# Attention spread between the matmuls of the FFN, in a fixed order, instead of all attention first

## The chip, the cores and the metric

The kernel runs on one core of one Trainium2 chip. The metric is the device time of one execution in microseconds; lower is better. Three runs of the kernel before are known, and one further execution was recorded by the profiler.

## The reference

The input has 4 batches, 8 heads, 768 positions and 64 channels a head, all fp32. Attention is linear, with a decay `lam` per head and a running state, and its result (3,072 tokens of 512 channels) goes through a bilinear FFN:

```python
for b in range(nb):                        # blocks of positions
    intra = einsum('bhic,bhjc->bhij', qb, kb) * Dmask      # Dmask: lam ** (i - j), 0 above the diagonal
    intra = einsum('bhij,bhjd->bhid', intra, vb)
    inter = einsum('bhid,bhde->bhie', qb * lam_pow, kv_state)
    out[:, :, sl] = intra + inter
    kv_state = lam_block * kv_state + einsum('bhsd,bhse->bhde', kb * rev_pow, vb)
...
x = out.transpose(0, 2, 1, 3).reshape(3072, 512)
return ((x @ w_a) * (x @ w_b)) @ w_out     # w_a, w_b: 512 x 1536, w_out: 1536 x 512
```

Both kernels take blocks of 128 positions and put the decay into the operands: q is scaled by `lam ** (pos + 1)` and k by `lam ** -(pos + 1)`, so that the mask is a plain triangle (`lotri`) and the state needs no decay.

## The kernel before

It has two stages, one after the other, and the framework's scheduler chooses the order of the instructions on each engine from the data they need and the buffers that are free.

The weights are loaded as fp32 by SyncE's queue (L88: four pieces of 768 KB each for `w_a` and `w_b`, twelve of 256 KB for `w_out`) and cast to bf16 by VectorE (L89). q, k and v are loaded by POOL's queue (L109 to L111), one DMA per batch, tensor and block of 128 positions, and cast from fp32 to bf16 by the DMA itself: it reads 256-byte rows (64 channels of one head and position) and writes 128-byte rows.

Attention then runs batch by batch. VectorE scales all q and all k of a batch (L115, L116, 3,072 elements a partition). TensorE transposes them in pairs of heads (L130, L131), and ScalarE copies eight transposes at once out of PSUM (L132). For each block and each pair of heads the inner loop multiplies k and q of one head (L152, `kq_ps`), VectorE masks the 128x128 result (L154), and TensorE adds up the block's own part (L156) and the state's part (L157) in `o_ps`; L158 makes the state's update, VectorE adds it to a bf16 state in SBUF (L160), and ScalarE copies `o_ps` into `xT_sb` (L161), which holds all 3,072 tokens. TensorE's matmuls of this loop have four shapes: 64x128, 128x64, 64x64 and again 128x64.

Last comes the FFN, for 6 groups of 512 tokens. For each of 12 chunks of 128 hidden channels TensorE does four matmuls into `a_ps` (L185) and four into `b_ps` (L188), all of 512 columns; ScalarE copies a (L191), VectorE multiplies it by b (L193), and four more matmuls (L195) add the chunk to four PSUM banks of output, open over all 12 chunks. At a group's end ScalarE copies the four banks into two SBUF buffers in turn (L199), and SyncE's queue stores them (L200).

Of the kernel before, what the change touches and what calls it, by code (L numbers as in the profile page):

```python
# [20 lines left out]


@with_exitstack
def kernel(
# [13 lines left out]
    assert D == 64  # L38
# [2 lines left out]
    d_model = moe_w_a.shape[0]
    d_ff = moe_w_a.shape[1]
# [1 line left out]
    assert d_model == H * D

    singles = ctx.enter_context(tc.tile_pool(name="singles", bufs=1))

    lam_bc = bass.AP(tensor=lam.tensor, offset=lam.offset, ap=[[0, 128], lam.ap[0]])
    lam_sb = singles.tile([128, H], F32, name="lam_sb")
    nc.sync.dma_start(out=lam_sb, in_=lam_bc)  # L50
# [27 lines left out]
    wa_sb = singles.tile([128, 4, d_ff], BF16, name="wa_sb")
    wb_sb = singles.tile([128, 4, d_ff], BF16, name="wb_sb")
    wo_sb = singles.tile([128, d_ff // 128, d_model], BF16, name="wo_sb")  # L80
    wtmp_pool = ctx.enter_context(tc.tile_pool(name="wtmp", bufs=3))
    for (src, dst, kdim, ndim) in ((moe_w_a, wa_sb, 4, d_ff),
                                   (moe_w_b, wb_sb, 4, d_ff),
                                   (moe_w_out, wo_sb, d_ff // 128, d_model)):
        src_r = src.rearrange("(ko p) n -> p ko n", p=128)
        for ki in range(kdim):
            wtmp = wtmp_pool.tile([128, ndim], F32, name="wtmp", tag="w")
            nc.sync.dma_start(out=wtmp, in_=src_r[:, ki, :])  # L88
            nc.vector.tensor_copy(dst[:, ki, :], wtmp)  # L89

    xT_sb = singles.tile([128, 4, N_TOK], BF16, name="xT_sb")

    qc = q.rearrange("b h (nb p) d -> b p nb h d", p=BLK)
    kc = k.rearrange("b h (nb p) d -> b p nb h d", p=BLK)
    vc = v.rearrange("b h (nb p) d -> b p nb h d", p=BLK)

    attn_ctx = ExitStack()
    bpool = attn_ctx.enter_context(tc.tile_pool(name="bpool", bufs=2))
    kvpool = attn_ctx.enter_context(tc.tile_pool(name="kvpool", bufs=2))
    blk_pool = attn_ctx.enter_context(tc.tile_pool(name="blk", bufs=4))  # L100
    psum1 = attn_ctx.enter_context(tc.tile_pool(name="psum1", bufs=1, space=bass.MemoryType.PSUM))
    psum2 = attn_ctx.enter_context(tc.tile_pool(name="psum2", bufs=2, space=bass.MemoryType.PSUM))

    for b in range(B):
        q_sb = bpool.tile([128, NB, H, 64], BF16, name="q_sb", tag="q")
        k_sb = bpool.tile([128, NB, H, 64], BF16, name="k_sb", tag="k")
        v_sb = bpool.tile([128, NB, H, 64], BF16, name="v_sb", tag="v")
        for nb in range(NB):
            nc.gpsimd.dma_start(out=q_sb[:, nb], in_=qc[b, :, nb])  # L109
            nc.gpsimd.dma_start(out=k_sb[:, nb], in_=kc[b, :, nb])  # L110
            nc.gpsimd.dma_start(out=v_sb[:, nb], in_=vc[b, :, nb])  # L111

        qs_sb = bpool.tile([128, NB, H, 64], BF16, name="qs_sb", tag="qs")
        ks_sb = bpool.tile([128, NB, H, 64], BF16, name="ks_sb", tag="ks")
# [2 lines left out]
        kv_sbs = []
        for hp in range(H // 2):
            kv = kvpool.tile([128, 64], BF16, name="kv", tag=f"kv{hp}")
            nc.vector.memset(kv, 0.0)  # L120
            kv_sbs.append(kv)

        qkT_all = bpool.tile([128, NB, 8, 128], BF16, name="qkT_all", tag="qkT")
        tr_ctx = ExitStack()
        psumT = tr_ctx.enter_context(tc.tile_pool(name="psumT", bufs=2, space=bass.MemoryType.PSUM))
        for nb in range(NB):
            tps = psumT.tile([128, 8, 128], BF16, name="tps", tag="T")
            for hp in range(H // 2):
                h0 = 2 * hp
                nc.tensor.transpose(tps[:, hp * 2, :], qs_sb[:, nb, h0:h0 + 2, :], ident)  # L130
                nc.tensor.transpose(tps[:, hp * 2 + 1, :], ks_sb[:, nb, h0:h0 + 2, :], ident)  # L131
            nc.scalar.copy(qkT_all[:, nb], tps)  # L132
        tr_ctx.close()

        for nb in range(NB):
            cols = slice(b * S + nb * BLK, b * S + (nb + 1) * BLK)
            for hp in range(H // 2):
                h0 = 2 * hp
                kv_sb = kv_sbs[hp]
                qT = qkT_all[:, nb, hp * 2, :]  # L140
                kT = qkT_all[:, nb, hp * 2 + 1, :]

                o_ps = psum2.tile([128, 128], F32, name="o_ps", tag="o")
                kvd_ps = psum1.tile([128, 64], F32, name="kvd_ps", tag="kvd")
                for i in range(2):
                    h = h0 + i
                    psl = slice(i * 64, (i + 1) * 64)
                    vb = v_sb[:, nb, h]
                    kb = ks_sb[:, nb, h]

                    kq_ps = psum1.tile([128, 128], F32, name="kq_ps", tag=f"kq{i}")
                    nc.tensor.matmul(kq_ps, lhsT=kT[psl, :], rhs=qT[psl, :], start=True, stop=True)  # L152
                    masked = blk_pool.tile([128, 128], BF16, name="masked", tag="msk")
                    nc.vector.tensor_mul(masked, kq_ps, lotri)  # L154

                    nc.tensor.matmul(o_ps[psl, :], lhsT=vb, rhs=masked, start=True, stop=False)  # L156
                    nc.tensor.matmul(o_ps[psl, :], lhsT=kv_sb[psl, :], rhs=qT[psl, :], start=False, stop=True)  # L157
                    nc.tensor.matmul(kvd_ps[psl, :], lhsT=kb, rhs=vb, start=True, stop=True)  # L158

                nc.vector.tensor_add(kv_sb, kv_sb, kvd_ps)  # L160
                nc.scalar.copy(xT_sb[:, hp, cols], o_ps)  # L161

    attn_ctx.close()

    fpsum = ctx.enter_context(tc.tile_pool(name="fpsum", bufs=1, space=bass.MemoryType.PSUM))
    ab_pool = ctx.enter_context(tc.tile_pool(name="ab", bufs=2))
    opool = ctx.enter_context(tc.tile_pool(name="opool", bufs=2))

    N_GROUP = 512
    NG = N_TOK // N_GROUP  # L170
    NT_SUB = N_GROUP // 128
    FF_CHUNKS = d_ff // 128
    K_SUB = d_model // 128
    out_r = out.rearrange("(g t p) n -> g t p n", p=128, t=NT_SUB)

    for g in range(NG):
        tok_sl = slice(g * N_GROUP, (g + 1) * N_GROUP)
        out_ps = [fpsum.tile([128, d_model], F32, name=f"out_ps{t}", tag=f"ops{t}")
                  for t in range(NT_SUB)]
        a_ps = fpsum.tile([128, N_GROUP], F32, name="a_ps", tag="aps")  # L180
        b_ps = fpsum.tile([128, N_GROUP], F32, name="b_ps", tag="bps")
        for f in range(FF_CHUNKS):
            fsl = slice(f * 128, (f + 1) * 128)
            for s in range(K_SUB):
                nc.tensor.matmul(a_ps, lhsT=wa_sb[:, s, fsl], rhs=xT_sb[:, s, tok_sl],  # L185
                                 start=(s == 0), stop=(s == K_SUB - 1))
            for s in range(K_SUB):
                nc.tensor.matmul(b_ps, lhsT=wb_sb[:, s, fsl], rhs=xT_sb[:, s, tok_sl],  # L188
                                 start=(s == 0), stop=(s == K_SUB - 1))
            a_sb = ab_pool.tile([128, N_GROUP], BF16, name="a_sb", tag="a")  # L190
            nc.scalar.copy(a_sb, a_ps)  # L191
            ab_sb = ab_pool.tile([128, N_GROUP], BF16, name="ab_sb", tag="ab")
            nc.vector.tensor_mul(ab_sb, a_sb, b_ps)  # L193
# [37 lines left out]
```

## Time and profile before

| | |
|---|---|
| median of 3 runs | 434.49 us (431.78 to 438.37) |
| span of the profiled execution, its own time | 432.4 us |
| TensorE matmuls busy | 362.2 us, 1,824 of them |
| VectorE, ScalarE, POOL busy | 163.2, 106.7, 66.5 us |
| DMA | 25.49 MB in 81,384 packets |

The profile gives no further time for the profiled execution than its span, from the first to the last instruction. The median of the runs lies 2.1 us above it. TensorE's busy time counts a matmul from its start to the end of its way through the array, so matmuls that overlap count as one stretch, and a busy TensorE isn't one at its peak: the distance between the starts of two matmuls tells more.

### The profile page before, as it was taken

To read this page: it belongs to the slowest core of one execution; us is meant where nothing else is said; L and a number is where in the kernel's file an instruction comes from. 1 tells how busy PE (TensorE), PEld (TensorE's weight loads), DVE (VectorE), ACT (ScalarE), POOL (GpSimd) and SP (SyncE) were. 2 spreads that over 40 slices of the span, in tenths; PEclk is the share of its full clock that TensorE was granted. 3 is DMA by queue.
4 is the path that set the end of the run, shared out by engine and by line. 5 is a ranking of instruction groups with operands and counts; after the bars stand their busy time and mean duration, and the time that the engine had idled before them with its cause. 6 is when DMAs were issued, how large, how long until landed. Compare 5 with 4: busy or idle time off the path is not lost.

```text
span 432.4 us, 4890 instructions
## 1 busy us (share of the span) xinstructions
PE 362.2 (84%) x1824; PEld 170.2 (39%) x1824; DVE 163.2 (38%) x406; ACT 106.7 (25%) x221; POOL 66.5 (15%) x81
## 2 busy tenths in 40 slices
PE   0000479957999999799999999999999999999993
PEld 0000345526655555455543333333333333333340
DVE  3325345588555555634432222222222222222220
ACT  3000411116511111151112213224224224213222
POOL 8458770049000400000000000000000000000000
PEclk9999999999555555555559999999999999999997
DMA  9999999059500920000000002002002002002002
GB/s 241 315 274 153 222 186 68 0 37 147 39 0 2 58 17 0 2 0 2 0 0 2 0 2 97 0 2 98 0 2 97 0 2 97 2 0 98 2 0 98
DMA packets 81384, 25.49 MB, mean 59 GB/s; under 512 B 75728, under 2 KB 75728, under 8 KB 81360
## 3 DMA queue, kind: packets, MB, share of 16 engines
q0 software_dynamic: 74880, 9.44, 35.6%
q1 hardware_dynamic: 6480, 15.74, 10.0%
q8 instruction: 14, 0.23, 0.2%
q14 instruction: 10, 0.08, 0.1%
HBM read 28.32 MB, written 6.29 MB: 80 GB/s over the span
## 4 chain that ended last, share of the span: by engine, by line
PE 80%; DMA 11%; DVE 3%; POOL 2%; issue 2%; ACT 1%; DVEq 0%; ACTq 0%; POOLq 0%
PE out_ps L195 17%; PE a_ps L185 15%; PE b_ps L188 15%; PE o_ps L157 10%; PE kq_ps L152 9%; PE o_ps L156 8%; DMA v_sb<-in_v_dram 4%; DMA wtmp<-in_moe_w_out_dram 4%; PE kvd_ps L158 4%; DMA k_sb<-in_k_dram 2%; PE tps L130 2%; DVE ks_sb L116 2%; PE tps L131 1%; ACT qkT_all L132 1%; POOL k_sb L110 1%
## 5 line engine op out<-in xcount | busy, mean ns | idle before, releaser
L193 DVE TENSOR_TENSOR ab_sb<-a_sb,b_ps 128x512 bf16<-128x512 bf16 x72 | 49.5, 688 | 151.5 <-PE b_ps L188 151.5
L191 ACT CAST a_sb<-a_ps 128x512 bf16<-128x512 f32 x72 | 42.2, 586 | 146.4 <-PE a_ps L185 146.4
L185 PE MATMUL a_ps<-xT_sb,wa_sb 128*128 128x512 bf16 x288 | 77.3, 386 | 0.3 <-DVE kv L160 0.3
L195 PE MATMUL out_ps<-wo_sb,ab_sb 128*128 128x512 bf16 x288 | 75.6, 382 | 1.2 <-DVE ab_sb L193 1.2
L188 PE MATMUL b_ps<-xT_sb,wb_sb 128*128 128x512 bf16 x288 | 74.8, 383 | 0.0
L154 DVE TENSOR_TENSOR masked<-kq_ps,lotri 128x128 bf16<-128x128 f32 x192 | 54.9, 291 | 46.1 <-PE kq_ps L152 45.3
L156 PE MATMUL o_ps<-masked,v_sb 128*64 128x128 bf16 x192 | 58.1, 302 | 4.8 <-DVE masked L154 4.8
L157 PE MATMUL o_ps<-qkT_all,kv 64*64 64x128 bf16 x192 | 59.6, 310 | 0.0
L130 PE MATMUL tps<-ident,qs_sb 128*128 128x128 bf16 x96 | 20.8, 293 | 45.0 <-DVE qs_sb L115 43.1
L152 PE MATMUL kq_ps<-qkT_all 64*128 64x128 bf16 x192 | 51.6, 283 | 0.4 <-DVE masked L154 0.4
L161 ACT CAST xT_sb<-o_ps 128x128 bf16<-128x128 f32 x96 | 25.5, 268 | 105.4 <-PE o_ps L157 105.4
L195 PEld LDWEIGHTS <-ab_sb 128*128 128x128 bf16 x288 | 22.4, 98 | 53.0 <-DVE ab_sb L193 35.6
L185 PEld LDWEIGHTS <-wa_sb 128*128 128x128 bf16 x288 | 28.4, 99 | 35.1 <-issue 1.6
L188 PEld LDWEIGHTS <-wb_sb 128*128 128x128 bf16 x288 | 28.4, 99 | 34.6 <-issue 1.1
L132 ACT COPY qkT_all<-tps 128x1024 bf16<-128x1024 bf16 x24 | 23.7, 1013 | 59.0 <-PE tps L131 58.9
L157 PEld LDWEIGHTS <-kv 64*64 64x64 bf16 x192 | 23.9, 124 | 27.1 <-issue 5.1
L111 POOL DMA_DIRECT2D v_sb<-in_v_dram x24 | 22.1, 931 | 65.5 <-PE o_ps L157 63.5
L156 PEld LDWEIGHTS <-v_sb 128*64 128x64 bf16 x192 | 26.6, 139 | 12.5 <-issue 1.5
L130 PEld LDWEIGHTS <-qs_sb 128*128 128x128 bf16 x96 | 12.4, 134 | 45.8 <-DVE qs_sb L115 43.2
L160 DVE TENSOR_TENSOR kv<-kv,kvd_ps 128x64 bf16<-128x64 bf16 x96 | 21.1, 220 | 24.1 <-PE o_ps L157 23.0
L131 PE MATMUL tps<-ident,ks_sb 128*128 128x128 bf16 x96 | 20.8, 297 | 9.9 <-DVE ks_sb L116 9.9
L152 PEld LDWEIGHTS <-qkT_all 64*128 64x128 bf16 x192 | 18.5, 102 | 21.6 <-issue 1.1
(28 smaller groups left out, 155.7 us busy)
## 6 DMA issues: line engine op xcount, KB each, us to landing
out_dram<-o_sb SPq DMA_DIRECT2D x24, 256.0 KB, 2.0
wtmp<-in_moe_w_a_dram SPq DMA_DIRECT2D x4, 768.0 KB, 7.2
q_sb<-in_q_dram POOLq DMA_DIRECT2D x24, 128.0 KB, 8.2
...
wtmp<-in_moe_w_out_dram SPq DMA_DIRECT2D x12, 256.0 KB, 6.0
lam_sb<-in_lam_dram SPq DMA_DIRECT2D x1, 4.0 KB, 2.7
```

Source lines behind the costliest of these rows:

```text
L130: nc.tensor.transpose(tps[:, hp * 2, :], qs_sb[:, nb, h0:h0 + 2, :], ident)
L132: nc.scalar.copy(qkT_all[:, nb], tps)
L152: nc.tensor.matmul(kq_ps, lhsT=kT[psl, :], rhs=qT[psl, :], start=True, stop=True)
L154: nc.vector.tensor_mul(masked, kq_ps, lotri)
L156: nc.tensor.matmul(o_ps[psl, :], lhsT=vb, rhs=masked, start=True, stop=False)
L157: nc.tensor.matmul(o_ps[psl, :], lhsT=kv_sb[psl, :], rhs=qT[psl, :], start=False, stop=True)
L161: nc.scalar.copy(xT_sb[:, hp, cols], o_ps)
L185: nc.tensor.matmul(a_ps, lhsT=wa_sb[:, s, fsl], rhs=xT_sb[:, s, tok_sl], start=(s == 0), stop=(s == K_SUB - 1))
L188: nc.tensor.matmul(b_ps, lhsT=wb_sb[:, s, fsl], rhs=xT_sb[:, s, tok_sl], start=(s == 0), stop=(s == K_SUB - 1))
L191: nc.scalar.copy(a_sb, a_ps)
L193: nc.vector.tensor_mul(ab_sb, a_sb, b_ps)
L195: nc.tensor.matmul(out_ps[t], lhsT=ab_sb[:, t * 128:(t + 1) * 128], rhs=wo_sb[:, f, :], start=(f == 0), stop=(f == FF_CHUNKS - 1))
```

## The change

The two stages become one. Attention works on units of one block of 128 positions with all 8 heads (24 units), and the units of the next 512 tokens are put between the FFN matmuls of the current 512 by a plan written out by hand; the scheduler is switched off (`manual_schedule`), so each engine's order is the program's order. Units 0 to 3 come before the first FFN matmul. The FFN of a group has two phases: first all a, b and products of the 12 chunks, kept in SBUF (`ab`), then for each 128 tokens 12 matmuls into one bank. A hook after each chunk (slots 0 to 11) and each half of an output tile (slots 12 to 19) issues the pieces of the next group's units.

q, k and v are loaded as fp32 by SyncE's queue, batch 0 block by block (256 KB), the others in one DMA per tensor. POOL scales q and k (for the first four units VectorE scales q), VectorE casts v (ScalarE for the first four). The weights come in nine chunks of 1 MB on the same queue, through three buffers, cast by VectorE, ScalarE and POOL. The state of a batch is added up in a PSUM bank of its own and copied to bf16 once per unit. One pool of seven PSUM banks serves everything else.

```diff
+    wst_pool = ctx.enter_context(tc.tile_pool(name="wst", bufs=3))
+    ld_pool = ctx.enter_context(tc.tile_pool(name="ld", bufs=2))
+    prep_pool = ctx.enter_context(tc.tile_pool(name="prep", bufs=4))
+    qkT_pool = ctx.enter_context(tc.tile_pool(name="qkT", bufs=3))
+    msk_pool = ctx.enter_context(tc.tile_pool(name="msk", bufs=2))
...
+    a_pool = ctx.enter_context(tc.tile_pool(name="a", bufs=3))
+    ab_pool = ctx.enter_context(tc.tile_pool(name="ab", bufs=2))
+    o_pool = ctx.enter_context(tc.tile_pool(name="o", bufs=4))
+    ps_pool = ctx.enter_context(tc.tile_pool(name="ps", bufs=7, space=PSUM))
+    kvps_pool = ctx.enter_context(tc.tile_pool(name="kvps", bufs=1, space=PSUM))
+
+    ctx.enter_context(tc.manual_schedule())
...
+    def load_batch(b, n0=0, n1=NB):
+        if b not in batch_tiles:
+            alloc_batch(b)
+        for t, src in zip(batch_tiles[b], (qr, kr, vr)):
+            if n0 == 0 and n1 == NB:
+                nc.sync.dma_start(out=t[:].rearrange("p h nb d -> p (h nb) d"),
+                                  in_=src[b].rearrange("p h nb d -> p (h nb) d"))
+            else:
+                for nb in range(n0, n1):
+                    nc.sync.dma_start(out=t[:, :, nb, :], in_=src[b, :, :, nb, :])
...
+    load_batch(0, 0, UPG)
+    load_w("a", 0)
+    load_w("b", 0)
+    load_w("a", 1)
...
-        nc.vector.tensor_mul(qs_sb, q_sb, lp_q_bc)
-        nc.vector.tensor_mul(ks_sb, k_sb, lp_k_bc)
+    def prep(u, first=False):
...
+        (nc.vector if first else nc.gpsimd).tensor_mul(qs, qf[:, :, nb, :], lq)
+        nc.gpsimd.tensor_mul(ks, kf[:, :, nb, :], lk)
+        if first:
+            nc.scalar.copy(vb, vf[:, :, nb, :])
+        else:
+            nc.vector.tensor_copy(vb, vf[:, :, nb, :])
...
+    def piece_T(u):
+        tps = ps_bank("tps", [128, 2, HP, 128], BF16)
+        for j, src in enumerate((d["qs"], d["ks"])):
+            for hp in range(HP):
+                nc.tensor.transpose(tps[:, j, hp, :], src[:, 2 * hp:2 * hp + 2, :], ident)
+        qkT = qkT_pool.tile([128, 2, HP, 128], BF16, name="qkT", tag="qkT")
+        nc.scalar.copy(qkT, tps)
+    def piece_KQ(u):
+        kq = [ps_bank(f"kq{i}", [128, HP, 128], F32) for i in range(2)]
+        for hp in range(HP):
+            for i in range(2):
+                p = slice(64 * i, 64 * i + 64)
+                nc.tensor.matmul(kq[i][:, hp, :], lhsT=qkT[p, 1, hp, :], rhs=qkT[p, 0, hp, :], ...
+        for i in range(2):
+            nc.vector.tensor_mul(m, kq[i], lotri_bc)
...
+    def piece_O(u, xT, col):
+        # hp, i: o_ps[p, hp] = vb (128x64) on m[i]; then, if nb > 0, += st (64x64) on qkT
+        nc.scalar.copy(xT[:, :, col:col + BLK], o_ps)
+        # if nb < NB - 1: hp, i: kvd[p, hp] += ks (128x64) on vb
+            nc.vector.tensor_copy(st, kvd)
...
+    def ffn(g, xT, hook):
+        ab = ab_pool.tile([128, FC, GT], BF16, name="ab", tag="ab")
+        for f in range(FC):
+            # 4 matmuls into a_ps, nc.scalar.copy(a_sb, a_ps), 4 into b_ps
+            nc.vector.tensor_mul(ab[:, f, :], a_sb, b_ps)
+            hook(f)
+        for t in range(UPG):
+            op = ps_bank("op", [128, d_model], F32)
+            for f in range(FC):
+                nc.tensor.matmul(op, lhsT=ab[:, f, t * 128:(t + 1) * 128], rhs=wo_sb[:, f, :],
+                                 start=(f == 0), stop=(f == FC - 1))
+                if f == FC // 2 - 1:
+                    hook(FC + 2 * t)
+            nc.scalar.copy(o_sb, op)
+            nc.sync.dma_start(out=out_r[g * UPG + t], in_=o_sb)
+            hook(FC + 2 * t + 1)
...
+    for u in range(UPG):
+        prep(u, first=True)
+    cast_w("a", 0, "dve")
+    cast_w("b", 0, "act")
+    load_w("b", 1)
+    load_w("a", 2)
+    load_batch(0, UPG, NB)
+    for step in range(UPG + 2):
+        if step < UPG:
+            piece_T(step)
+        if 0 <= step - 1 < UPG:
+            piece_KQ(step - 1)
+        if 0 <= step - 2 < UPG:
+            piece_O(step - 2, xTs[0], (step - 2) * BLK)
+    base = [0, 4, 9, 14]
+    offs = [(1, 2, 4), (1, 2, 4), (1, 2, 3), (1, 2, 3)]    # slots of T, K, O of the next group's four units
+    preps = {0: 0, 3: 1, 8: 2, 12: 3}
...
+            if g == 0:
+                if slot == 0:
+                    cast_w("a", 1, "dve")
+                    load_w("b", 2)
+                if slot == 1:
+                    cast_w("b", 1, "act")
+                    load_w("o", 0)
+                if slot == 3:
+                    cast_w("a", 2, "dve")
+                    load_w("o", 1)
+                if slot == 4:
+                    cast_w("b", 2, "act")
+                    load_w("o", 2)
+                    load_batch(1)
+                # slots 7, 9, 10: cast_w("o", 0 / 1 / 2, "pool")
+            if slot in preps:
+                u = nxt * UPG + preps[slot]
+                prep(u)
+                if u % NB == NB - 1 and u // NB + 2 < B:
+                    load_batch(u // NB + 2)
```

## Rows read from the trace of the kernel before

**Rows 1.** The page: span, and the chain that ended last, by engine.

```profile
span 432.4 us, 4890 instructions
...
PE 80%; DMA 11%; DVE 3%; POOL 2%; issue 2%; ACT 1%; DVEq 0%; ACTq 0%; POOLq 0%
```

**Rows 2.** Windows: stretch, length, busy us (count) per engine, granted clock, DMA share, GB/s.

```profile
0.00:40.40 40.40, 0.03 (x1) 0.03 (x2) 12.72 (x21) 3.26 (x5) 26.11 (x36) 1.00 1.60 252
40.40:223.50 183.10, 161.32 (x960) 90.92 (x960) 100.87 (x314) 48.75 (x120) 40.40 (x46) 0.69 0.64 48
223.50:228.80 5.30, 5.21 (x13) 1.92 (x14) 0.72 (x2) 0.59 (x1) 0.00 (x0) 0.50 0.00 0
229.00:425.60 196.60, 195.39 (x852) 77.31 (x850) 48.85 (x71) 52.37 (x93) 0.00 (x0) 1.00 0.07 27
425.60:432.40 6.80, 0.07 (x1) 0.00 (x0) 0.00 (x0) 1.71 (x4) 0.00 (x0) 0.60 0.41 155
```

**Rows 3.** Timeline of TensorE from 309.8 us: start, length, instruction.

```profile
309.89 1.03 PE L188 MATMUL b_ps<-xT_sb,wb_sb 128*128 128x512 bf16 x4
310.75 1.03 PE L185 MATMUL a_ps<-xT_sb,wa_sb 128*128 128x512 bf16 x4
311.77 0.60 PE L195 MATMUL out_ps<-wo_sb,ab_sb 128*128 128x512 bf16 x2
```

**Rows 4.** Timeline of TensorE from 45 us.

```profile
45.31 0.31 PE L130 MATMUL tps<-ident,qs_sb 128*128 128x128 bf16 x1
45.41 0.31 PE L131 MATMUL tps<-ident,ks_sb 128*128 128x128 bf16 x1
```

**Rows 5.** Timeline of TensorE from 102.6 us.

```profile
102.86 0.22 PE L131 MATMUL tps<-ident,ks_sb 128*128 128x128 bf16 x1
102.92 0.22 PE L130 MATMUL tps<-ident,qs_sb 128*128 128x128 bf16 x1
...
103.30 0.24 PE L157 MATMUL o_ps<-qkT_all,kv 64*64 64x128 bf16 x1
103.47 0.24 PE L156 MATMUL o_ps<-masked,v_sb 128*64 128x128 bf16 x1
...
103.81 0.23 PE L152 MATMUL kq_ps<-qkT_all 64*128 64x128 bf16 x2
103.97 0.23 PE L130 MATMUL tps<-ident,qs_sb 128*128 128x128 bf16 x1
```

**Rows 6.** Timeline from 223.5 us, the first matmuls of the FFN.

```profile
223.59 1.89 PE L185 MATMUL a_ps<-xT_sb,wa_sb 128*128 128x512 bf16 x4 [0.32 <-DVE kv L160]
...
225.27 1.91 PE L188 MATMUL b_ps<-xT_sb,wb_sb 128*128 128x512 bf16 x4
```

**Rows 7.** The page's costliest groups: busy us, mean ns of one, idle before and releaser.

```profile
L193 DVE TENSOR_TENSOR ab_sb<-a_sb,b_ps 128x512 bf16<-128x512 bf16 x72 | 49.5, 688 | 151.5 <-PE b_ps L188 151.5
L191 ACT CAST a_sb<-a_ps 128x512 bf16<-128x512 f32 x72 | 42.2, 586 | 146.4 <-PE a_ps L185 146.4
...
L132 ACT COPY qkT_all<-tps 128x1024 bf16<-128x1024 bf16 x24 | 23.7, 1013 | 59.0 <-PE tps L131 58.9
...
L111 POOL DMA_DIRECT2D v_sb<-in_v_dram x24 | 22.1, 931 | 65.5 <-PE o_ps L157 63.5
```

**Rows 8.** Groups of instructions by line, shapes apart: weight cast, POOL's select.

```profile
L89 DVE CAST wa_sb<-wtmp 128x1536 bf16<-128x1536 f32 x4 | 4.1, 1014 | 10.3 <-DMA wtmp<-in_moe_w_a_dram 10.3
...
L58 POOL TENSOR_SCALAR_AFFINE_SELECT lotri<-lotri 128x128 bf16<-128x128 bf16 x1 | 0.3, 294 | 0.0
```

**Rows 9.** DMA: window of weight loads; POOL's queue (packets, MB, share); store's landing.

```profile
4.00:8.00 4.00, 0.00 (x0) 0.00 (x0) 0.96 (x1) 1.03 (x1) 4.00 (x5) 1.00 1.02 383
...
q0 software_dynamic: 74880, 9.44, 35.6%
...
out_dram<-o_sb SPq DMA_DIRECT2D x24, 256.0 KB, 2.0
```

**Rows 10.** Timeline of the end: the last two copies and their wait.

```profile
427.95 1.20 ACT L199 COPY o_sb<-out_ps 128x512 f32<-128x512 f32 x2 [1.82 <-DMA out_dram<-o_sb]
```

More of the change, by code (lines that the diff above doesn't have):

```diff
@@ L37 @@
     B, H, S, D = q.shape
[L38 removed]
     BLK = 128
     NB = S // BLK
[L41 to L42 removed]
+    HP = H // 2
+    d_model, d_ff = moe_w_a.shape
+    assert D == 64 and d_model == H * D
     N_TOK = B * S
[L44 to L50 removed]
+    GT = 512
@@ L78 @@
[L78 to L114, printed above, removed]
-        nc.vector.tensor_mul(qs_sb, q_sb, lp_q_bc)
-        nc.vector.tensor_mul(ks_sb, k_sb, lp_k_bc)
[L117 to L144, printed above, removed]
-                for i in range(2):
[L146 to L174, printed above, removed]
-    for g in range(NG):
[L177 to L193, printed above, removed]
-            for t in range(NT_SUB):
-                nc.tensor.matmul(out_ps[t], lhsT=ab_sb[:, t * 128:(t + 1) * 128],
-                                 rhs=wo_sb[:, f, :], start=(f == 0), stop=(f == FF_CHUNKS - 1))
-        for t in range(NT_SUB):
-            o_sb = opool.tile([128, d_model], F32, name="o_sb", tag="osb")
-            nc.scalar.copy(o_sb, out_ps[t])
-            nc.sync.dma_start(out=out_r[g, t], in_=o_sb)
@@ new lines, in piece_O @@
+    def piece_O(u, xT, col):
+        b, nb = divmod(u, NB)
+        d = U.pop(u)
+        ks, vb, qkT, m = d["ks"], d["vb"], d["qkT"], d["m"]
+        o_ps = ps_bank("o_ps", [128, HP, 128], F32)
+        for hp in range(HP):
+            for i in range(2):
+                p = slice(64 * i, 64 * i + 64)
+                nc.tensor.matmul(o_ps[p, hp, :], lhsT=vb[:, 2 * hp + i, :], rhs=m[i][:, hp, :],
+                                 start=(hp == 0), stop=(nb == 0), skip_group_check=True)
+        if nb > 0:
+            st = kv_state[b]
+            for hp in range(HP):
+                for i in range(2):
+                    p = slice(64 * i, 64 * i + 64)
+                    nc.tensor.matmul(o_ps[p, hp, :], lhsT=st[p, hp, :], rhs=qkT[p, 0, hp, :],
+                                     start=False, stop=True, skip_group_check=True)
+        nc.scalar.copy(xT[:, :, col:col + BLK], o_ps)
+        if nb < NB - 1:
+            if nb == 0:
+                kv_state["ps"] = kvps_pool.tile([128, HP, D], F32, name="kvd", tag="kvd")
+            kvd = kv_state["ps"]
+            for hp in range(HP):
+                for i in range(2):
+                    p = slice(64 * i, 64 * i + 64)
+                    nc.tensor.matmul(kvd[p, hp, :], lhsT=ks[:, 2 * hp + i, :], rhs=vb[:, 2 * hp + i, :],
+                                     start=(nb == 0 and hp == 0), stop=True, skip_group_check=True)
+            st = kv_pool.tile([128, HP, D], BF16, name="st", tag="st")
+            nc.vector.tensor_copy(st, kvd)
+            kv_state[b] = st
@@ new lines @@
+    out_r = out.rearrange("(t p) n -> t p n", p=128)
+    def ffn(g, xT, hook):
+        ab = ab_pool.tile([128, FC, GT], BF16, name="ab", tag="ab")
+        for f in range(FC):
+            fsl = slice(f * 128, (f + 1) * 128)
+            a_ps = ps_bank("a_ps", [128, GT], F32)
+            for s in range(KS):
+                nc.tensor.matmul(a_ps, lhsT=wa_sb[:, s, fsl], rhs=xT[:, s, :],
+                                 start=(s == 0), stop=(s == KS - 1))
+            a_sb = a_pool.tile([128, GT], BF16, name="a_sb", tag="a")
+            nc.scalar.copy(a_sb, a_ps)
+            b_ps = ps_bank("b_ps", [128, GT], F32)
+            for s in range(KS):
+                nc.tensor.matmul(b_ps, lhsT=wb_sb[:, s, fsl], rhs=xT[:, s, :],
+                                 start=(s == 0), stop=(s == KS - 1))
+            nc.vector.tensor_mul(ab[:, f, :], a_sb, b_ps)
[7 more added lines that the diff above has]
+                    hook(FC + 2 * t)
+            o_sb = o_pool.tile([128, d_model], F32, name="o_sb", tag="osb")
+            nc.scalar.copy(o_sb, op)
+            nc.sync.dma_start(out=out_r[g * UPG + t], in_=o_sb)
+            hook(FC + 2 * t + 1)
```

119 lines of the change are left out of this document (107 added, 12 removed).

## The prediction, on record before the change was built

> **What bounds the kernel now.** I read the span and the chain of waits first [rows 1]: the chain that ended last is TensorE for 80% and DMA for 11%. The windows of the five stages [rows 2] show why. For 40.4 us nothing but loading happens. From 40.4 to 223.5 us attention runs by itself: TensorE is shown busy for 161 of 183 us, but with 128-column matmuls that wait on each other. From 223.5 us on the FFN runs; one slow stretch of 5.3 us at clock 0.50, then 196.6 us at 1.00, then 6.8 us of last copies and stores. In the FFN a chunk of 12 matmuls lasts 2.75 us: four take 0.86 us (0.2155 us each, 309.89 to 310.75), and after the a_ps matmuls 0.16 us is lost before out_ps starts (310.75 to 311.77 is 1.02) [rows 3]. So FFN matmuls are near their pace; what can go is the 183 us of attention by itself, some loading, and 72 x 0.16 = 12 us of waiting for ab_sb.
>
> What attention costs TensorE is read from pitches, not busy time. Transposes, all of one shape, start 0.107 us apart at 45 us [rows 4] and 0.055 us at 102.9 us [rows 5]: 128 columns at 1.2 and at 2.4 GHz. The clock of 1.00 in the first window [rows 2] therefore isn't a measured grant: until about 102.5 us the engine ran at the lower level. At the higher level, where the shape changes at each step (128x64, 64x64, 64x128), starts are 0.17 us apart, while two kq_ps matmuls of one shape on different row halves take one such step together (103.81 to 103.97) [rows 5]. The change sorts by shape, so this row matters most.
>
> **The change, part by part.**
>
> FFN: 864 matmuls stay. In two phases no out_ps matmul waits for its own chunk's ab: 864 x 0.2155 = **186.2 us** [rows 3]. The first ones run at 1.2 GHz: four took 1.68 us at the start of the old FFN, which lasted 5.3 us at 0.50 [rows 2, 6]; I take the same loss, **2.6 us**.
>
> Attention of 20 of the 24 units lies between FFN matmuls. Per unit: 8 transposes x 0.055 = 0.44; KQ, O and state each four pairs x 0.055 = 0.66; state update four pairs of half that = 0.12; six changes of shape (into and out of KQ, into O, to the state product, to the update, back) x 0.17 = 1.0. That is 2.2 us, and 20 x 2.2 = **44 us**. Ends: 1.6 if part of a change hides, 3.0 if the 28 matmuls don't pair; 6.1 if each of 36 costs 0.17.
>
> Does this stay TensorE's bound? Per group of about 41 us, VectorE has 12 x 0.69 for ab [rows 7], and per unit two masks of that size (eight of the old 128x128 products in two instructions), a v cast and a state copy, under 2.3 us: 17 us. ScalarE has 12 x 0.59, 4 x (1.01 + 0.59), 4 x 0.59: 16 us [rows 7]. POOL has eight multiplies a group. No row has one; POOL's 128x128 select took 0.29 us [rows 8], four times the elements about 1.2, at worst double: 10 to 20 us a group, ahead of use. Their cover is the FFN; without it they would cost what the startup shows. Two gaps aren't covered: in phase 2 the slots are six matmuls (1.3 us) apart, and a unit's KQ needs its 1.01 us copy, its O two masks (1.4 us) plus latencies. I charge 1 us per group, **5 us**.
>
> Startup: all loads now sit in SP's queue, in program order: 12 of 256 KB (1,024 rows of 256 B each), then the 1 MB chunks a0, b0, a1. Prices: the weights moved at 383 GB/s [rows 9], so 2.75 us per MB. For 256-byte rows written as fp32 there is no row. POOL's DMAs read the same 256-byte rows (and wrote 128 B [rows 9]) at 1,024 per 0.93 us [rows 7], 1,100 rows/us, perhaps POOL's own issuing pace. Bounds: 1,490 rows/us (the weights' rate) and 500, under half of POOL's. I take 1,000, nearest to the row of the same reads, a little less since the written bytes double. Then 12 x 1.02 from about 2 us, with 2.0 us to landing [rows 9], has v3 at 15, a0 at 17.8, b0 at 20.5. The cast of b0 stands in ScalarE's queue **ahead** of the first qkT copy, and the cast of a0 in VectorE's ahead of the first mask: ScalarE needs 4 x 0.43 us (from 1.01 per 1,024 columns [rows 7]) and VectorE 1.3 (from 1.01 per 1,536 [rows 8]). First copy done at 23.6. Four units in a six-step pipeline at the lower clock then take about 2 us a step (KQ 0.6, two masks 1.4, O and state 1.5, copy 0.6, partly over each other), 11 us: FFN starts at **34.7 us** instead of 223.5.
>
> The new wait is in group 0. In slot 3 the preparation of unit 5 (last of batch 0) issues load_batch(2); load_batch(1) comes in slot 4, **behind** it on SP. Unit 6, in slot 8, is batch 1. Slot 3 is reached at 34.7 + 10 = 45 us (four chunks of 1.73, the first two nearly doubled, plus T and K), the cast of a2 then frees o1's buffer: o1 lands at 50. Batch 2 is 18,432 rows, 18.4 us: 68.4. o2: 71. Batch 1: q at 77, k at 83.4, v at 89.5. POOL's ks multiply waits for k, so TensorE meets T of unit 6 (slot 10, reached at 60.5) with nothing to do until 84.5: **24 us**. VectorE stands in front of v's cast until 89.5 with three ab products and two masks queued behind it, which TensorE's phase 2 and O need: 2 us. After such a gap I take the clock to be at the lower level again, as it was after the old start's 40 us without work [rows 2, 4], and 2.6 us goes once more: together **4.6 us**. POOL's wo casts (o1, o2) are queued behind that ks multiply too; at four times the select per 512 columns, 3 to 5 us each, they end near 92, just in time for phase 2. Group 0's stores queue behind batch 1 and wait for nobody. Later load_batch(3), issued in group 1, has 60 us.
>
> Tail: the old end waits 1.82 us for an output buffer and copies two more tiles [rows 10]; with four buffers and one tile left, 6.8 becomes about **3.9 us**.
>
> Sum: 34.7 + 186.2 + 2.6 + 44 + 5 + 24 + 4.6 + 3.9 = **305 us** of span, against 432.4. The runs' median is 434.49, 2.1 above that span, so **307 us**.
>
> **A rule against the change.** The weights' 383 GB/s come from rows of 2 KB and more; the 256-byte rows of POOL ran slower than that [rows 7, 9]. If the fp32 rows ran at half the weights' rate, 745 rows/us, each 256 KB would take 1.38 us: 12 x 0.36 = 4 at the start and 2 x 6.3 in group 0, 324 us in all. The Trainium skill, "DMA: Bandwidth & Descriptors", Specifications, asks for transfers of at least 512 B for line rate, since below that a read-modify-write takes place; by that rule this case comes out, and the trace, with about 1,100 such rows/us read, bears it out only in part.
>
> **Rivals.**
> (a) *Loads slower*: 745 to 500 rows/us. At 500 the start gains 12 us and the two batches 37: 354. For it: no row shows such writes. Against: POOL's pace. 324 to 354.
> (b) *No load wait*: SP issues the batches earlier than I think, or rows move much faster, so that batch 1 meets slot 8. 305 - 28.6 = 276, 279 with what lies outside the span. Against: 9.4 MB must move between about 47 us and slot 10 at 60.
> (c) *Matmuls don't pair*, each costs a change of shape: 20 x 3.9 = 78 more, 385. For it: 0.17 us is all that mixed shapes show. Against: the kq_ps pair.
> (d) *Slower*: the clock stays at 1.2 GHz in the mixed groups 0 to 4. For it: attention between 40.4 and 223.5 us averaged 0.69, with the higher figure from the unmeasured start, though TensorE looked 88% busy [rows 2]. 720 x (0.42 - 0.2155) = 147 and attention some 40 more: 494. It is slower than before once two thirds of that stretch is at the lower level. Against: three quarters of each group is the very matmul stream that held 1.00 for 196 us.
>
> **How the numbers follow.** Forecast 0.62; (a) 0.23; (b) 0.07; (c) 0.05; (d) 0.03. The unit's ends (1.6 to 3.0) are 12 us down and 16 up; faster rows (1,490) 16 down. The forecast's own range is 284 to 325; to 345 it takes in most of (a). Left out are (b), the top of (a), (c) and (d): 0.19. Faster by over 2% (about what a measurement can tell from no change): all but (d) and some mishap, 0.96; within 2% 0.01; slower 0.03.
>
> **What would show it.** FFN start at 33 to 40 us; a TensorE gap of over 15 us in group 0 that ends on k or v of batch 1, with batch 2's landing before; groups 1 to 4 of 40 to 42 us each at clock 1.00, group 5 of 31; KQ starts in pairs. A group over 45 us, clock 0.50 past 100 us, or no gap in group 0 would each prove a step wrong.

## The result and the profile after

The changed kernel takes 306.21 us (median of 4 runs, 306.06 to 306.61) against 433.13 us (4 runs, 431.61 to 438.37) for the kernel before: ratio 0.707, 95% interval 0.7036 to 0.7104. The forecast was 307, with the same mechanism. Its terms did not come out as written, though: load waits cost 12 us more than predicted, and three other terms 13 us less, so it is luck that the sum came this close.

The page's span and its chain by engine, against [rows 1]:

```profile
span 304.6 us, 4308 instructions
...
PE 66%; SPq 16%; DMA 8%; DVE 5%; issue 2%; ACT 2%; DVEq 0%; ACTq 0%
```

TensorE still holds most of the chain, but a quarter now is SP's queue and transfers, which held 11% before. The windows say where. Columns as in [rows 2]: stretch, length, busy us (count) of PE, PE's weight loads, VectorE, ScalarE, POOL; granted clock, DMA share, GB/s. The cuts are at the first FFN matmul of each group and around the gap of group 0.

```profile
0.00:35.08 35.08, 10.16 (x153) 7.43 (x153) 10.56 (x18) 13.71 (x18) 6.43 (x14) 1.00 1.11 268
35.08:58.10 23.02, 22.67 (x160) 10.73 (x159) 13.29 (x19) 12.79 (x17) 5.91 (x4) 1.00 0.89 239
58.10:92.10 34.00, 1.13 (x9) 0.73 (x9) 0.00 (x0) 0.00 (x0) 2.52 (x3) 0.55 1.10 231
92.10:114.80 22.70, 18.84 (x123) 8.14 (x121) 7.38 (x11) 5.44 (x8) 13.69 (x12) 0.84 0.29 75
114.80:153.68 38.88, 38.74 (x297) 18.83 (x296) 15.67 (x27) 15.36 (x24) 8.30 (x8) 1.00 0.67 150
153.68:192.34 38.66, 38.52 (x297) 18.74 (x296) 16.00 (x28) 15.36 (x24) 8.34 (x8) 1.00 0.07 29
...
269.64:300.88 31.24, 31.24 (x145) 13.99 (x143) 8.25 (x12) 9.36 (x16) 0.00 (x0) 1.00 0.09 34
300.88:304.60 3.72, 0.00 (x1) 0.00 (x0) 0.00 (x0) 0.59 (x1) 0.00 (x0) 0.93 0.18 70
...
60.90:68.50 7.60, 0.00 (x0) 0.00 (x0) 0.00 (x0) 0.00 (x0) 0.00 (x0) 0.56 1.11 218
```

Groups 1 to 4 take 38.88, 38.66, 38.42 and 38.88 us (mean 38.71), and group 5, FFN alone, 31.24: so the next group's attention costs 7.5 us, where all six groups' took 183 by itself [rows 2]. Group 0 takes 79.7 us. In its middle, 34 us long, almost nothing is computed; from 60.9 to 68.5 every busy figure is zero, while data move at 218 GB/s, against 383 for the weights [rows 9].

What ended the gap stands in brackets in TensorE's timeline (start, length, instruction, [idle before it <- what ended that]). The first row is the start of the FFN; the others lie in the gap and behind it:

```profile
35.08 1.02 PE L242 MATMUL a_ps<-xT,wa_sb 128*128 128x512 bf16 x4 [0.43 <-ACT xT L219]
...
84.48 0.61 PE L182 MATMUL tps<-ident,qs 128*128 128x128 bf16 x4 [26.24 <-POOL qs L169]
91.72 0.61 PE L182 MATMUL tps<-ident,ks 128*128 128x128 bf16 x4 [6.63 <-POOL ks L170]
92.12 1.91 PE L242 MATMUL a_ps<-xT,wa_sb 128*128 128x512 bf16 x4
...
101.07 0.24 PE L210 MATMUL o_ps<-m,vb 128*64 128x128 bf16 x1 [3.51 <-DVE m L199]
...
102.10 5.75 PE L255 MATMUL op<-wo_sb,ab 128*128 128x512 bf16 x18
```

TensorE waited for POOL's two multiplies, and POOL in turn waited for transfers, as did VectorE's cast of v. POOL's timeline, then VectorE's:

```profile
83.39 1.04 POOL L169 TENSOR_TENSOR qs<-qf,lp_q 128x512 bf16<-128x512 f32 x1 [33.85 <-DMA qf<-in_q_dram]
90.62 1.04 POOL L170 TENSOR_TENSOR ks<-kf,lp_k 128x512 bf16<-128x512 f32 x1 [6.20 <-DMA kf<-in_k_dram]
```

```profile
97.47 1.15 DVE L174 CAST vb<-vf 128x512 bf16<-128x512 f32 x1 [42.68 <-DMA vf<-in_v_dram]
98.54 1.87 DVE L250 TENSOR_TENSOR ab<-a_sb,b_ps 128x512 bf16<-128x512 bf16 x3
100.33 1.27 DVE L199 TENSOR_TENSOR m<-kq,lotri 128x512 bf16<-128x512 f32 x2
```

The landings of q, k and v are 7.23 and 6.85 us apart. Each is 6,144 rows of 256 B: 850 to 900 rows/us, where I took 1,000. VectorE's cast stood 42.7 us in front of three ab products and two masks, just the queue that was predicted for it. SP's queue gives the order (start, length until the queue had taken the DMA, instruction):

```profile
45.98 0.82 SPq L92 DMA_DIRECT2D qf<-in_q_dram  x1
47.25 8.94 SPq L92 DMA_DIRECT2D kf<-in_k_dram  x1
...
63.49 7.06 SPq L109 DMA_DIRECT2D wst<-in_moe_w_out_dram  x1
70.77 0.70 SPq L92 DMA_DIRECT2D qf<-in_q_dram  x1
```

First come the three tensors of one batch (v at 56.64, left out), then o2, then q, k and v once more. The second three are those whose landing at 83.39, 90.62 and 97.47 ended the waits: batch 2 went ahead of batch 1.

Inside a group, one stretch of phase 1 and one unit of phase 2 (TensorE's timeline, columns as above):

```profile
157.13 0.39 PE L182 MATMUL tps<-ident,qs 128*128 128x128 bf16 x4
...
157.58 1.03 PE L242 MATMUL a_ps<-xT,wa_sb 128*128 128x512 bf16 x4
158.44 1.03 PE L248 MATMUL b_ps<-xT,wb_sb 128*128 128x512 bf16 x4
159.40 0.40 PE L194 MATMUL kq<-qkT 64*128 64x128 bf16 x8
159.73 1.04 PE L242 MATMUL a_ps<-xT,wa_sb 128*128 128x512 bf16 x4
...
180.05 0.77 PE L210 MATMUL o_ps<-m,vb 128*64 128x128 bf16 x8
180.75 0.41 PE L217 MATMUL o_ps<-qkT,st 64*64 64x128 bf16 x8
...
188.80 0.43 PE L210 MATMUL o_ps<-m,vb 128*64 128x128 bf16 x8
189.15 0.41 PE L217 MATMUL o_ps<-qkT,st 64*64 64x128 bf16 x8
189.49 0.32 PE L227 MATMUL kvd<-vb,ks 128*64 128x64 bf16 x8
189.74 2.76 PE L255 MATMUL op<-wo_sb,ab 128*128 128x512 bf16 x12
```

Eight transposes take 0.45 us (157.13 to 157.58), the same pitch as in [rows 5]. Eight KQ matmuls take 0.33, and 0.10 is lost ahead of them: the four b_ps before would end their turn at 158.44 + 0.86 = 159.30. O, state product and update take 0.35, 0.34 and 0.25 (188.80, 189.15, 189.49, 189.74), with 0.11 ahead of them in the same way. A full unit costs 0.45 + 0.43 + 1.05 = 1.93 us; as the first block of a batch has no state product and the last no update, the mean is 1.93 - (0.34 + 0.25) / 6 = 1.83. The unit at 180.05 shows the wait that I had charged for phase 2: its O takes 0.70 to the state product instead of 0.35.

### The profile page after: what moved, and what is told of

It is laid out like the page before. It is cut to its first block, busy times and chain, and to the rows that moved or that the text cites. A ratio compares the mean times of both kernels' runs of the same rounds, so it can differ in the third digit from the quotient of the medians.

```text
span 304.6 us, 4308 instructions
## 1 busy us (share of the span) xinstructions
PE 238.3 (78%) x1760; PEld 116.0 (38%) x1760; DVE 102.6 (34%) x168; ACT 103.3 (34%) x156; POOL 53.5 (18%) x56
## 4 chain that ended last, share of the span: by engine, by line
PE 66%; SPq 16%; DMA 8%; DVE 5%; issue 2%; ACT 2%; DVEq 0%; ACTq 0%
PE op L255 19%; PE a_ps L242 18%; PE b_ps L248 17%; SPq L92 9%; DMA vf<-in_v_dram 5%; SPq L96 4%; PE tps L182 3%; DVE m L199 3%; DMA wst<-in_moe_w_b_dram 3%; PE o_ps L210 2%; SPq L109 2%; PE kq L194 2%; PE o_ps L217 2%; PE kvd L227 1%; DVE ab L250 1%
## 5 line engine op out<-in xcount | busy, mean ns | idle before, releaser
L250 DVE TENSOR_TENSOR ab<-a_sb,b_ps 128x512 bf16<-128x512 bf16 x72 | 49.3, 687 | 86.0 <-PE b_ps L248 85.8
L242 PE MATMUL a_ps<-xT,wa_sb 128*128 128x512 bf16 x288 | 75.0, 383 | 0.4 <-ACT xT L219 0.4
L248 PE MATMUL b_ps<-xT,wb_sb 128*128 128x512 bf16 x288 | 74.8, 383 | 0.0
L255 PE MATMUL op<-wo_sb,ab 128*128 128x512 bf16 x288 | 68.3, 387 | 0.0
L245 ACT CAST a_sb<-a_ps 128x512 bf16<-128x512 f32 x72 | 42.2, 587 | 58.3 <-PE a_ps L242 58.3
L199 DVE TENSOR_TENSOR m<-kq,lotri 128x512 bf16<-128x512 f32 x48 | 30.8, 683 | 35.2 <-PE kq L194 35.1
L184 ACT COPY qkT<-tps 128x1024 bf16<-128x1024 bf16 x24 | 24.2, 1013 | 45.1 <-PE tps L182 45.1
L169 POOL TENSOR_TENSOR qs<-qf,lp_q 128x512 bf16<-128x512 f32 x20 | 20.8, 1041 | 102.1 <-PE tps L182 49.7
L255 PEld LDWEIGHTS <-ab 128*128 128x128 bf16 x288 | 26.7, 99 | 30.9 <-issue 2.3
L170 POOL TENSOR_TENSOR ks<-kf,lp_k 128x512 bf16<-128x512 f32 x24 | 26.3, 1098 | 65.9 <-PE kvd L227 39.3
L260 ACT COPY o_sb<-op 128x512 f32<-128x512 f32 x24 | 14.0, 585 | 46.8 <-PE op L255 46.8
L174 DVE CAST vb<-vf 128x512 bf16<-128x512 f32 x20 | 10.8, 540 | 42.7 <-DMA vf<-in_v_dram 42.7
L194 PEld LDWEIGHTS <-qkT 64*128 64x128 bf16 x192 | 5.8, 99 | 23.6 <-ACT qkT L184 16.8
```

The lines of the kernel that those rows point to most:

```text
L170: nc.gpsimd.tensor_mul(ks, kf[:, :, nb, :], lk)
L184: nc.scalar.copy(qkT, tps)
L194: nc.tensor.matmul(kq[i][:, hp, :], lhsT=qkT[p, 1, hp, :], rhs=qkT[p, 0, hp, :], start=True, stop=True, skip_group_check=True)
L199: nc.vector.tensor_mul(m, kq[i], lotri_bc)
L242: nc.tensor.matmul(a_ps, lhsT=wa_sb[:, s, fsl], rhs=xT[:, s, :], start=(s == 0), stop=(s == KS - 1))
L248: nc.tensor.matmul(b_ps, lhsT=wb_sb[:, s, fsl], rhs=xT[:, s, :], start=(s == 0), stop=(s == KS - 1))
```

## Experiments

Theory at the start: group 0's gap is the time of 256-byte rows, paid twice because batch 2 is loaded ahead of batch 1; attention between FFN matmuls is cheap because matmuls on the two halves of the array run at the same time. E1 to E4 ran on one chip beside the kernel before, which took 434.28 us there, and E5 to E8 on another, where it took 434.07; ratios are to the kernel before on the same chip. E1, E3, E4 and E7 start from the changed kernel, E2 from E1, and E5, E6 and E8 from E2.

**E1, batch 1 first.** Only the order on SP's queue:

```diff
+                if slot == 12:
+                    load_batch(2)
...
-                if u % NB == NB - 1 and u // NB + 2 < B:
+                if u % NB == NB - 1 and u // NB + 2 < B and g > 0:
                     load_batch(u // NB + 2)
```

> Batch 1 is loaded in slot 4 of group 0 as before, batch 2 only in slot 12, behind it. Theory (the order of the two batch loads makes TensorE's gap in group 0): a batch takes 21.7 us at the 217 GB/s seen in the changed kernel, so k and v of batch 1 land some 22 to 28 us earlier (k near 64 us, v near 70 us, instead of 91 and 97 us), the gap of 34 us shrinks to 5 to 8 us, and the time falls to 277 to 284 us. Rival (the gap comes from something else, PSUM banks or POOL's queue): the gap stays above 25 us and the time above 298 us.

285.62 us, ratio 0.6578 (0.654 to 0.6616): 20.6 us less than the changed kernel, though 1.6 above the range expected. POOL's timeline of E1:

```profile
62.08 1.04 POOL L169 TENSOR_TENSOR qs<-qf,lp_q 128x512 bf16<-128x512 f32 x1 [12.28 <-DMA qf<-in_q_dram]
69.19 1.04 POOL L170 TENSOR_TENSOR ks<-kf,lp_k 128x512 bf16<-128x512 f32 x1 [6.07 <-DMA kf<-in_k_dram]
```

q is there 21.3 us earlier than at 83.39, just batch 2's 18,432 rows at 850 to 900 rows/us. The order theory holds, but the expectation of k at 64 us was too early: it took off more than the 21.7 us that a batch lasts. What stays is a second gap: k follows q by 7.1 us, since a whole tensor must land before its first block is used, and TensorE still waits some 11.5 us where 5 to 8 were expected.

**E2, the first two blocks of batch 1 ahead of the rest.** As E1, and:

```diff
-                    load_batch(1)
+                    load_batch(1, 0, 2)
+                    load_batch(1, 2, NB)
```

> As the first kernel, but batch 1 is loaded block by block, and the two blocks that group 0 needs (6 x 256 KB, 7.2 us at 1.19 us each) come ahead of the other four. Theory (what group 0 waits for is only the landing of these blocks): k lands near 54 us and v near 57 us, before TensorE reaches slot 10 at 58 us; the gap is under 2 us, the clock never falls after the start, and the time is 264 to 272 us. Rival (a gap of its own cause remains, or the weights o1 and o2 take its place): over 275 us.

268.13 us, ratio 0.6174 (0.6138 to 0.621), as expected. TensorE's timeline of E2 has the same transposes as in the gap above:

```profile
57.94 0.39 PE L182 MATMUL tps<-ident,qs 128*128 128x128 bf16 x4
59.37 0.40 PE L182 MATMUL tps<-ident,ks 128*128 128x128 bf16 x4 [1.05 <-POOL ks L170]
```

26.24 and 6.63 us of waiting became none and 1.05, and the granted clock is 1.00 in the whole span. (POOL's multiply of k starts at 58.3 and VectorE's cast of v at 60.5, some 4 us later than expected, but TensorE hardly notices.) Group 0 lasts 41.0 us (34.93 to 75.92) instead of 79.7, within 2.3 us of the groups behind it. So order and cut of the batch loads, with the same bytes moved, account for 38.7 us of group 0 and 38.1 us of the whole time.

**E3, 1,536-byte rows**, and **E7, 512-byte rows**, for batches 1 to 3; the order stays that of the changed kernel:

```diff
+    q6 = q.rearrange("b h (p nb) d -> b p h (nb d)", nb=NB)                # E3
+    q2 = q.rearrange("b h (o p w) d -> b p h o (w d)", p=BLK, w=2)         # E7
...
-                nc.sync.dma_start(out=t[:].rearrange("p h nb d -> p (h nb) d"),
-                                  in_=src[b].rearrange("p h nb d -> p (h nb) d"))
+                nc.sync.dma_start(out=t[:].rearrange("p h nb d -> p h (nb d)"), in_=src6[b])
```

> Batches 1 to 3 are loaded in rows of 1,536 bytes (a partition holds six neighbouring positions), in the order of the changed kernel; which positions form a block changes, so the output differs. Bytes are the same, rows are a sixth. Theory (the loads are paced by the number of rows that SyncE's queue issues, 850 a microsecond): a tensor of 1.57 MB moves at the weights' 383 GB/s, 4.1 us instead of 7.2, batch 2 and batch 1 together save 18 to 19 us, time 285 to 290 us. Rival (fp32 into many partitions moves at 217 GB/s whatever the rows): time stays 303 to 308 us.

> As the changed kernel, but batches 1 to 3 are loaded in rows of 512 bytes (a partition holds two neighbouring positions); which positions form a block changes, so the output differs. Theory (a row under 512 bytes pays a penalty, one of 512 none): 370 to 385 GB/s, 4.2 us a tensor, time 286 to 290 us as with rows of 1,536 bytes. Rival (each row pays a fixed 8 ns beside its bytes, as worked out from 13.9 ns for 128-byte and 18.8 ns for 256-byte writes): 280 GB/s, 5.6 us a tensor, time 294 to 298 us.

E3: 287.31 us, ratio 0.6613 (0.6579 to 0.6648). E7: 293.83 us, ratio 0.6787 (0.6754 to 0.6819). POOL's timelines of E3, then of E7:

```profile
71.70 1.04 POOL L173 TENSOR_TENSOR qs<-qf,lp_q 128x512 bf16<-128x512 f32 x1 [21.90 <-DMA qf<-in_q_dram]
75.94 1.04 POOL L174 TENSOR_TENSOR ks<-kf,lp_k 128x512 bf16<-128x512 f32 x1 [3.20 <-DMA kf<-in_k_dram]
```

```profile
76.23 1.04 POOL L173 TENSOR_TENSOR qs<-qf,lp_q 128x512 bf16<-128x512 f32 x1 [26.64 <-DMA qf<-in_q_dram]
81.67 1.04 POOL L174 TENSOR_TENSOR ks<-kf,lp_k 128x512 bf16<-128x512 f32 x1 [4.40 <-DMA kf<-in_k_dram]
```

The same 1.57 MB land 7.23 us after q in 256-byte rows, 5.44 in 512-byte rows and 4.24 in 1,536-byte rows. That is 218, 289 and 371 GB/s, and the windows of loading show 218, 290 and 374. Both kernels put other positions into a block, so their output is another one, and they count for the pace of their loads alone. With bytes, order and queue the same, the pace follows the length of the rows (and with it their number); E3 hit its range, and in E7 the theory that 512 bytes are enough for full pace fell and the rival (a fixed time per row) came nearest. If the rows are spread evenly over the 16 engines of the profile, a row takes 16 x 256 / 218 = 18.8 ns at 256 B, 28.2 at 512 B and 65.7 at 1,536 B: an estimate from these of roughly 9 ns and 0.037 ns per byte fits all three. The Trainium skill, "DMA: Bandwidth & Descriptors", Specifications, puts the least size for line rate at 512 B; here 512-byte rows reached 290 GB/s and the weights' 383 [rows 9], so the measurement decides against it.

**E4, v over POOL's queue.**

```diff
-                nc.sync.dma_start(out=t[:].rearrange("p h nb d -> p (h nb) d"),
-                                  in_=src[b].rearrange("p h nb d -> p (h nb) d"))
+                eng = nc.gpsimd if src is vr else nc.sync
+                eng.dma_start(out=t[:].rearrange("p h nb d -> p (h nb) d"),
+                              in_=src[b].rearrange("p h nb d -> p (h nb) d"))
```

> v of batches 1 to 3 goes over POOL's queue, q and k stay on SyncE's; rows of 256 bytes, order as in the changed kernel. Theory (each queue issues at its own pace, and the DMA engines could take more than 850 rows a microsecond): both queues together move over 1,300 rows a microsecond, k of batch 1 lands near 80 us instead of 91, v is there before it, and the time falls to 286 to 294 us. Rival (the engines or the memory set the pace of such rows): the sum of both stays near 850 to 900 rows a microsecond, k lands at 88 us or later, time 302 to 308 us.

308.84 us, ratio 0.7101 (0.7063 to 0.7138): no gain, and the theory of a pace for each queue, which wanted over 1,300 rows/us, fell. SP's timeline of E4, then a window of it:

```profile
47.36 23.90 SPq L93 DMA_DIRECT2D kf<-in_k_dram  x1
```

```profile
52.00:56.00 4.00, 4.00 (x32) 1.86 (x31) 1.56 (x3) 1.51 (x4) 0.00 (x0) 1.00 1.05 258
```

The queue took batch 2's k in 23.9 us instead of 8.9, and both queues together moved 258 GB/s (248 from 60 to 64 us) instead of 218. That is 970 to 1,010 rows/us, 14 to 18% above one queue's 850 and somewhat more than the rival's 850 to 900. So most of the limit lies in what both queues share, and v's rows, sent at once, delayed the q and k that TensorE waits for (first transposes of unit 6 at 91.95 instead of 84.48).

**E5, no pairs in program order.** In KQ, O, state product and update all four matmuls of one half stand ahead of the four of the other:

```diff
-        for hp in range(HP):
-            for i in range(2):
+        for i in range(2):
+            for hp in range(HP):
```

> As the kernel with batch 1's two blocks first (268 us), but in KQ, O, state and update the four matmuls of one half follow each other (i outside, hp inside), so that no two neighbours can run side by side. Theory (neighbours on different halves run as pairs, and that is why a unit takes only 1.8 us): KQ, O and state 0.22 us longer each, the update 0.1, so 0.75 us a unit, 15 to 18 us in all: 283 to 287 us, groups 1 to 4 at 41.5 to 42 us instead of 38.7. Rival (a matmul of half the array costs half without a partner, or weight loads set the pace in either order): under 272 us.

268.61 us, ratio 0.6195 (0.617 to 0.6219), against 268.13 for E2: no change, where the theory wanted 15 us or more. TensorE's timeline of E5, the KQ in the slot of the one at 159.40 above, but a group later:

```profile
159.74 0.41 PE L194 MATMUL kq<-qkT 64*128 64x128 bf16 x8
```

The single starts in the trace are 159.740, .753, .806, .819, .861, .875, .917 and .931. The second of them already bears the wait on the other half's bank, which the program issues fifth. So the two halves run side by side whatever their order in the program, 13 ns apart here and 3 ns in pairs. The overlap that the theory needs is there in both kernels; what fell is that it hangs on the order in the program. The edit thus didn't keep the halves apart, and what attention would cost without the overlap no run shows. The Trainium skill, "TensorEngine Tiling (Array Packing)", Key Properties, says that tiles operate independently and that a change of mode drains TensorE; the trace agrees with the first, and for the second shows the 0.10 us ahead of KQ.

**E6, attention not spread.** The next group's four units stand in one block behind each group's FFN:

```diff
-            for name, kk in plan.get(slot, ()):
+            for name, kk in ():
...
         ffn(g, xTs[g], hook)
+        if nxt < NG:
+            for step in range(UPG + 2):
+                if step < UPG:
+                    piece_T(nxt * UPG + step)
+                if 0 <= step - 1 < UPG:
+                    piece_KQ(nxt * UPG + step - 1)
+                if 0 <= step - 2 < UPG:
+                    piece_O(nxt * UPG + step - 2, xTs[nxt], (step - 2) * BLK)
```

> As the kernel with batch 1's two blocks first (268 us), but the four units of the next group run in one piece behind each group's FFN, in the six-step pipeline of the start, instead of between FFN matmuls. Theory (spreading hides the copies and masks): a block of four units takes 10 to 11 us instead of 7.3, so 13 to 18 us more over five groups, less what group 0 no longer waits for: 278 to 286 us, TensorE waiting on the qkT copy and on the masks in each block. Rival (the order of whole units is enough, spreading is worth nothing): 264 to 271 us. Second rival (the clock falls in each block): over 295 us.

283.17 us, ratio 0.6534 (0.6508 to 0.656): 15 us slower than E2, as expected, though only in part for the reason expected. TensorE's timeline of E6:

```profile
55.73 1.03 PE L255 MATMUL op<-wo_sb,ab 128*128 128x512 bf16 x4
60.98 1.22 PE L255 MATMUL op<-wo_sb,ab 128*128 128x512 bf16 x3 [4.22 <-POOL wo_sb L126]
...
74.34 0.39 PE L182 MATMUL tps<-ident,qs 128*128 128x128 bf16 x4
...
83.74 1.02 PE L242 MATMUL a_ps<-xT,wa_sb 128*128 128x512 bf16 x3 [0.43 <-ACT xT L219]
```

A block takes 9.4 us (74.34 to 83.74), not 10 to 11, against 7.5 spread, so about 2 us a group is gained by spreading. The rest is in group 0, 48.7 us (35.02 to 83.74) against 41.0 in E2: with no attention in its phase 1 TensorE comes to the output weights at 55.7, before they are there; some 6 of the 15 us come from this. Of the 166 us by which E2 beats the kernel before, the spreading is thus worth 15. The rest lies in attention sorted by shape, at the full clock and without the old loop's waits, and in the new startup and FFN; how it divides among them was not tried. Attention that isn't spread already is three times as fast: four units took 183 / 6 = 30.5 us in the old loop and take 9.4 in E6's block. The clock has a part in it, as the old loop ran at the lower level for most of its time (columns: stretch, length, TensorE busy, granted clock, DMA share, GB/s):

```profile
110.00:222.00 112.00, 108.52 (x619) 0.50 0.13 9
```

**E8, the startup cut as in E2.** The first group's blocks are loaded unit by unit and prepared step by step, the weight casts stand behind the first units, b's casts are halved over VectorE and ScalarE, and the later chunks are moved to later slots. Its core:

```diff
-    for u in range(UPG):
-        prep(u, first=True)
-    cast_w("a", 0, "dve")
-    cast_w("b", 0, "act")
...
     for step in range(UPG + 2):
         if step < UPG:
+            prep(step, first=True)
             piece_T(step)
...
+        if step == UPG:
+            cast_w("a", 0, "dve")
+            load_w("b", 1)
+    cast_w("b", 0, "both")
```

> As the kernel with batch 1's two blocks first (268 us); the first blocks are loaded unit by unit (q, k, v of one block), the casts of a0 and b0 come behind the first four units (b0's halves on VectorE and ScalarE), and the later weight chunks and blocks stand in the queue in the order of use. Theory (the FFN's start at 35 us is set by b0's cast ahead of the first copy, and after that the queue's 53 us of loading up to the last wo chunk is the bound): FFN starts at 25 to 27 us, phase 2 of group 0 waits for wo until about 57 us, and the time is 259 to 264 us. Rival (loading paces all of group 0, so an earlier start only waits later): 266 to 270 us.

263.18 us, ratio 0.6068 (0.604 to 0.6097), as expected, and the fastest here. The FFN starts at 25.78 us instead of 34.93, but group 0 lasts 44.6 us instead of 41.0 (next start 70.35): 9.2 gained, 3.6 given back. Its b_ps matmuls now wait 3.0 us in two places for casts of wb_sb (us in total, times, longest), and an out matmul 1.5 us for wo_sb:

```profile
PE b_ps L255 <- DVE wb_sb L125: 3.0, 2, 1.6
```

## Why the prediction was right, and what in it was wrong

The mechanisms held: group 0's gap with its cause and its queue, the rest of attention under the FFN, the clock at 1.00 in the mixed groups. No rival came true; slower rows (a) came nearest, as 850 to 900 rows/us lie between my 1,000 and its 745. (Its upper end of 354 leaves out the 2 us outside the span, which its 324 holds.) The total is this near because mis-sized terms cancel, and that is luck. Span, in us:

| step | predicted | measured | from |
|---|---|---|---|
| FFN start | 34.7 | 35.1 | first window |
| first FFN matmuls at half clock | 2.6 | 0 | 35.08: four take 0.86 (next row of the trace at 35.94) |
| FFN, 864 matmuls | 186.2 | 186.4 | group 5: 31.24 for 144, so 0.2 of waits there |
| attention of 20 units | 44 | 36.6 | 20 x 1.83 |
| phase-2 waits | 5 | 1.8 | 5 x (38.71 - 31.03 - 4 x 1.83) |
| gap and catch-up, group 0 | 28.6 | 41.0 | 79.72 - 38.71 |
| tail | 3.9 | 3.7 | last window |
| sum | 305.0 | 304.6 | |

The measured rows of phase-2 waits and of gap and catch-up are what is left of the groups' lengths, so the measured column adds up to the span by itself. Groups 1 to 4 lie at 38.4 to 38.9 us, below the 40 to 42 that I had set as a sign, through attention and these waits.

**Gap and catch-up, +12.4.** The step "I take 1,000, nearest to the row of the same reads" (rows/us) failed: 850 to 900. k of batch 1 was there at 90.6, not 83.4; some 5 us of that are three tensors of batch 2 and two of batch 1 at about 1 us more each; batch 2 also began some 2 us later than reckoned. The gap also began earlier, at 58.1 instead of 60.5, because the units and the first FFN matmuls ahead of it were cheaper. So it is 33.6 us without its transposes (34.02 - 0.45), not 24. Behind it, v came at 97.5 and held up TensorE until 101.07 (3.5 + 0.35 us of waits), and the clock cost more than the 2.6 I took: eight matmuls at 92.12 took 3.55 us and eighteen at 102.10 took 5.6, where 0.2155 each makes 1.72 and 3.88; that is 3.5 lost, with the waits 7.4, not 4.6. The granted clock was 0.50 from 92.12 to 95.68 and again from 102.8 to 106.0, after the wait for v (columns as in the windows above):

```profile
92.12:95.68 3.56, 3.56 (x12) 1.04 (x10) 0.00 (x0) 1.60 (x2) 3.56 (x3) 0.50 1.12 217
...
102.80:106.00 3.20, 3.20 (x9) 1.22 (x8) 0.34 (x2) 0.58 (x1) 0.90 (x1) 0.50 0.09 28
```

I had foreseen one such stretch, not a second; a clock of 0.50 past 100 us stood among the signs of a wrong step, and it is one.

**Attention, -7.4.** The step "six changes of shape x 0.17" counted something twice. The 0.17 us of [rows 5] is the distance from one start to the next, and it holds the 0.055 us of the matmul itself, which the unit's sum already had in its 1.22 us of matmuls. A change adds only 0.17 - 0.055 = 0.115 us, and so it was measured: a full unit's 1.93 less those 1.22 leaves 0.12 for each of the six. That is 0.27 of the 2.2; the other 0.10 is the state products and updates that the first and last block of a batch don't have and that I charged to every unit.

**First FFN matmuls, -2.6.** I took the loss of the old start, where attention alone came before and the granted clock was 0.50 [rows 2, 6]. Here the full clock was back before the FFN began, with nothing but attention ahead of it: eight KQ still took 0.54 us at 26.35 (0.33 at the full clock), but eight state products took 0.34 at 33.99, as at 189.15 at clock 1.00.

**Startup, a hit by two errors.** The cast of b0 indeed stood ahead of the first copy, and 256-byte rows at 218 GB/s made it later than predicted: ScalarE's timeline,

```profile
23.49 1.90 ACT L122 CAST wb_sb<-wst 128x2048 bf16<-128x2048 f32 x1 [4.80 <-DMA wst<-in_moe_w_b_dram]
25.29 1.92 ACT L184 COPY qkT<-tps 128x1024 bf16<-128x1024 bf16 x2
```

The first copy was done at 26.3, not 23.6, and the four units then took 8.8 us, not 11.

**Phase-2 waits, -3.2.** Only the first O of a phase waits, 0.35 us (180.05); the other slots are far enough apart.

**POOL** stayed covered: a multiply takes 1.04 us, not 1.2, eight a group 8.3 us (windows above). Its wo casts, queued behind ks, ran from 91.6 to 95.3, 1.9 us each where I took 3 to 5.

What the runs leave open: what the sorting by shape and the full clock are worth each by itself, and why the old loop stayed at 0.50 from 110 to 222 us while the startup's attention reached the full clock.
